# Instruction order and evacuation engines chosen per instruction, in a long-convolution and MLP kernel

## The chip, the cores and the metric

The kernel runs on one core of one Trainium2 chip. The metric is the device time of one launch in microseconds (us). A profile's span, from the first to the last instruction, is about 1.8 us shorter than the launch's time. All runs quoted here were in the fast state, and all gave the reference's result.

The names in the profiles: PE multiplies matrices, and PEld loads its weights; DVE, ACT and POOL work on vectors (ACT also computes the GELUs); SP issues most transfers, and SPq is its queue. SBUF is the core's working memory, and PSUM takes what PE writes. An evacuation is the copy of a result from PSUM to SBUF. A slab is 128 rows of the sequence. The granted clock is the share of its full speed that PE was allowed.

## The reference, cut to what matters

Sequence S = 2048, width D = 512, MLP width F = 1376, bf16.

```python
def A(q, k, v, shift_k, ssm_k, ssm_D):           # gated long convolution
    kv = shift_conv_4_taps(k, shift_k) * v
    y = irfft(rfft(pad(kv)) * rfft(pad(ssm_k)))[:S]
    return q * (y + kv * ssm_D)                  # y does not depend on q
def B(x): return gelu(layernorm(x) @ w1 + b1) @ w2 + b2

x = A_q
for layer in range(2):
    x = x + A(layernorm(x), k, v, ...)
    x = x + B(layernorm(x))
```

The convolution y is the same in both layers, so the kernel computes it once. Then come two layers of norms and MLP, all of them bound to PE.

## The kernel before

The program is recorded as a list of numbered operations. A list scheduler then fixes each engine's order (and the PSUM banks) before launch, from assumed durations. A last pass adds the semaphore waits. Operations carry tags: `ht` (transpose of the filter), `h1`, `h2` (the filter's transform, two stages), `fir*` (the four-tap convolution), `x1`, `x2` (transform of kv and the products of the spectra), `i1`, `i2` (inverse transform, two stages), `q`, `y`, `z` (norms and gate), `m1`, `m2` (MLP).

The scheduler's choice, cut:

```python
            o.ready = 0.0
    ...
            o.prio = o.base + o.extra + self.BIAS.get(o.tag, 0.0) + ...
    ...
            for e in free:                       # the five engines
                for o in ready[e]:
                    s = max(free[e], o.ready)    # and a free PSUM pair
                    k = (s + (self.SHY.get(o.tag, 300.0) if e == DVE and len(o.engs) > 1
                              and o.dur[DVE] > o.dur[ACT] else 0.0), -o.prio, o.i)
```

An evacuation of PSUM may run on ACT or on DVE (`BOTH`). The part that the argument turns on is the filter's spectrum, its copies and the products:

```python
    for k8 in range(16):                         # tag h2
        tl = stage2(R_G, range(8 * k8, 8 * k8 + 8), 128)      # 8 matmuls, 128 columns
        evac(BOTH, A(0, 128, R_H + 32 * k8, [4, 8], [512, 32], [1, 4]), ..., E1, tl)
    for d0, n in PARTS:                          # channels 0-63, then 64-127 of each block
        for g in range(2):
            for c in range(0, 128 * n, 2048):    # 16 copies of 256 KB, SBUF to SBUF
                src, dst = ...                   # partition halves swapped
                dma(dst, src, 1 << 18, reads=[src], rate=210.0)
    ...
            tt(h, x, h, ALU.mult, 30 + 1.09 * w) # a product: reads the spectrum and its copy
```

Each of the 16 h2 evacuations writes some columns of every channel, so each of the 16 copies reads what all 16 evacuations wrote.

## Time and profile before

| | us |
|---|---|
| time, median (lowest to highest, 3 runs; a fourth came with the result) | 247.12 (246.87 to 247.75) |
| span of the profiled run | 245.5 |
| first copy issued (end of h2) | 39.49 |
| second eight products start / end on DVE | 63.63 / 72.80 |
| inverse 2 starts on PE | 80.69 |
| first MLP matmul | 89.06 |
| last addition on DVE starts, lasts | 242.48, 0.69 |

The times from the first copy on are the joints of the chain: what lies between two of them can be compared from kernel to kernel even where the instructions are in another order. Two views that the prediction does not show follow. The first is DVE's order of time (start, duration, instructions, and in brackets the idle time before them with what ended it), at the second products:

```profile
63.63 9.17 DVE L513 TENSOR_TENSOR ar<-ar 128x2048 bf16<-128x2048 bf16 x8 [1.18 <-DMA ar<-ar]
```

DVE waits 1.18 us for a copy: up to there the copies, not DVE, set the pace. The second is PE's order of time where the convolution ends (L790 inverse 2, L884 the transposes of the first slab, L897 the MLP):

```profile
83.75 4.09 PE L790 MATMUL ps<-ar 128*128 128x256 bf16 x36
87.92 0.62 PE L884 MATMUL ps<-ar 128*128 128x128 bf16 x8
89.06 2.41 PE L897 MATMUL ps<-ar 128*128 128x128 bf16 x40 [0.52 <-DVE ar L519]
```

Here PE does two slabs' transposes in one piece after inverse 2, then waits 0.52 us for their evacuation on DVE.

### The profile page before, as it was taken

What the parts mean: (1) busy time and instruction counts of PE and PEld (TensorE: products, weight loads), DVE (VectorE), ACT (ScalarE), POOL (GpSimd) and SP (SyncE); (2) the same over time, 40 slices, a digit from 0 to 9 for tenths busy, and PEclk for the clock granted to TensorE, in tenths of its full rate; (3) what the DMA queues carried; (4) which work ended last, traced back from release to release, by engine and by line L of the source; (5) the groups of instructions that cost most, each with busy time, mean ns of one, the idle gap of its engine ahead of it and who ended that gap; (6) DMA issues with size and microseconds to landing.
All of it is one profiled execution on the core that took longest, in us unless ns stands there. A gap on an engine that the chain in (4) does not pass through costs nothing.

```text
span 245.5 us, 5643 instructions
## 1 busy us (share of the span) xinstructions
PE 228.3 (93%) x2382; PEld 154.6 (63%) x2399; DVE 175.1 (71%) x361; ACT 140.9 (57%) x222; POOL 34.1 (14%) x71
## 2 busy tenths in 40 slices
PE   7968789896799989999999999999999999999994
PEld 3857779785689878776586666744444444444443
DVE  0759999999898898889999967998687203002233
ACT  2297898999898997665455343633265130872000
POOL 2320002000003031232231111102121000000000
PEclk9999999999999999999999999999999999999999
DMA  6999923999996000420222023101520501101112
GB/s 240 372 408 406 406 47 82 215 212 212 346 396 198 0 3 0 45 43 3 46 43 43 3 41 67 24 1 21 101 53 0 109 19 43 45 0 43 43 45 85
DMA packets 25770, 27.68 MB, mean 113 GB/s; under 512 B 17585, under 2 KB 19984, under 8 KB 25616
## 3 DMA queue, kind: packets, MB, share of 16 engines
q1 hardware_dynamic: 25598, 27.21, 37.8%
q8 instruction: 19, 0.31, 0.5%
q10 hardware_dynamic: 146, 0.10, 0.2%
q14 instruction: 7, 0.06, 0.1%
HBM read 17.34 MB, written 2.10 MB: 79 GB/s over the span
## 4 chain that ended last, share of the span: by engine, by line
PE 64%; DVE 12%; SPq 8%; DMA 8%; issue 2%; ACT 2%; POOL 1%
PE ps L897 31%; PE ps L930 30%; SPq L502 8%; DVE ar L513 8%; DMA ar<-in_A_k_dram 5%; DMA ar<-ar 3%; DVE ar L519 2%; ACT ar L518 2%; PE ps L734 1%; PE ps L919 1%; POOL sm L830 1%; DVE sm L822 1%; PE ps L790 1%; DVE ar L672 1%; PE ps L623 0%
## 5 line engine op out<-in xcount | busy, mean ns | idle before, releaser
L902 ACT ACTIVATE ar<-ps,sm 128x256 bf16<-128x256 f32 (+5 forms) x143 | 67.1, 524 | 69.5 <-PE ps L930 55.1
L897 PE MATMUL ps<-ar 128*128 128x256 bf16 (+4 forms) x569 | 79.7, 297 | 0.7 <-DVE ar L519 0.5
L930 PE MATMUL ps<-ar 128*128 128x512 bf16 (+1 forms) x327 | 74.4, 379 | 0.7
L518 ACT ACTIVATE ar<-ps 128x1024 bf16<-128x1024 f32 (+1 forms) x76 | 71.4, 1038 | 6.4 <-PE ps L610 2.9
L897 PEld LDWEIGHTS ps<-ar 128*128 128x128 bf16 (+1 forms) x572 | 53.2, 100 | 26.9 <-DVE ar L519 0.7
L513 DVE TENSOR_TENSOR ar<-ar 128x512 bf16<-128x512 bf16 (+2 forms) x104 | 61.9, 642 | 3.3 <-DMA ar<-in_A_k_dram 1.8
L930 PEld LDWEIGHTS ps<-ar 128*128 128x128 bf16 (+1 forms) x341 | 33.2, 98 | 37.5
L934 DVE TENSOR_TENSOR ar<-ar,ps 128x512 bf16<-128x512 bf16 x31 | 20.6, 681 | 44.8 <-PE ps L930 44.8
L822 DVE BATCH_NORM_STATS2 sm<-ar 128x6 f32<-128x512 bf16 (+1 forms) x68 | 41.8, 647 | 0.0
L837 DVE TENSOR_SCALAR ar<-ar,sm 128x512 bf16<-128x512 bf16 x64 | 23.5, 403 | 8.6 <-POOL sm L830 8.6
L830 POOL TENSOR_TENSOR sm<-sm 128x2 f32<-128x2 f32 (+2 forms) x26 | 20.2, 778 | 2.2
L610 PE MATMUL ps<-ar 128*64 128x128 bf16 x512 | 17.7, 221 | 2.7 <-ACT ar L518 1.9
L519 DVE CAST ar<-ps 128x1024 bf16<-128x1024 f32 (+1 forms) x16 | 17.9, 1149 | 3.1 <-PE ps L610 1.6
L828 POOL TENSOR_SCALAR sm<-sm 128x2 f32<-128x2 f32 (+2 forms) x26 | 5.7, 218 | 92.2 <-DVE sm L824 92.0
L734 PE MATMUL ps<-ar 128*128 128x128 bf16 x256 | 15.3, 220 | 3.0 <-DVE ar L513 1.6
L610 PEld LDWEIGHTS ps<-ar 128*64 128x64 bf16 x512 | 14.8, 110 | 5.1 <-ACT ar L518 3.0
L734 PEld LDWEIGHTS ps<-ar 128*128 128x128 bf16 x256 | 14.6, 114 | 3.6 <-DVE ar L513 1.7
L519 DVE COPY ar<-ps 128x2048 bf16<-128x2048 bf16 (+1 forms) x8 | 7.1, 917 | 6.8 <-PE ps L593 6.8
L710 PE MATMUL ps<-ar 128*128 128x64 bf16 x256 | 9.4, 193 | 1.9 <-ACT ar L518 1.1
L824 DVE BATCH_NORM_AGGREGATE sm<-sm 128x2 f32<-128x6 f32 (+1 forms) x64 | 10.3, 173 | 0.2
L710 PEld LDWEIGHTS ps<-ar 128*128 128x128 bf16 x256 | 8.1, 98 | 3.1 <-ACT ar L518 2.2
L623 PE MATMUL ps<-ar 128*128 128x128 bf16 x128 | 8.4, 220 | 1.5 <-ACT ar L518 1.0
(30 smaller groups left out, 77.5 us busy)
## 6 DMA issues: line engine op xcount, KB each, us to landing
ar<-tab_s SPq DMA_DIRECT2D x8, 512.0 KB, 16.1
ar<-ar SPq DMA_DIRECT2D x16, 256.0 KB, 6.5
ar<-in_A_ssm_k_dram SPq DMA_DIRECT2D x4, 512.0 KB, 5.4
ar<-in_A_k_dram SPq DMA_DIRECT2D x4, 512.0 KB, 10.1
ar<-in_A_v_dram SPq DMA_DIRECT2D x4, 512.0 KB, 13.6
ar<-in_A_q_dram SPq DMA_DIRECT2D x4, 512.0 KB, 9.0
out_dram<-ar SPq DMA_DIRECT2D x7, 256.0 KB, 2.0
ar<-in_B_w_dram SPq DMA_DIRECT2D x1, 1376.0 KB, 12.5
```

The costliest lines, as they stand in the source:

```text
L513: return P.op(eng, lambda e: e.tensor_tensor(o, a, b, op), dur, reads=[a, b] + list(more), writes=[o])
L518: return e.activation(dst, src(), AF.Copy)
L519: return e.tensor_copy(dst, src())
L610: r = e.matmul(Q(tl, 64 * ri, 64, i * 128, [1, 128]), w, m, start=True, stop=True)
L734: r = e.matmul(Q(tl, 0, 128, i * 128, [1, 128]), w, m, start=q == 0, stop=q == 1)
L822: P.op(DVE, lambda e, sj=sj, x=x: e.bn_stats(sj, x), 40.0 + 1.1 * w, reads=[x], writes=[sj], gate=gate)
L830: P.op(POOL, lambda e: e.tensor_tensor(r, v, hf, ALU.pow), 430.0 + 150.0 * n, reads=[v, hf], writes=[r])
L837: P.op(DVE, lambda e: e.tensor_scalar(o, x, m, r, ALU.subtract, ALU.mult), 335.0, reads=[x, m, r], writes=[o])
L897: r = e.matmul(Q(tl, 0, rows, 0, [1, w]), a, m, start=dk == 0, stop=dk == 3)
L902: P.op(ACT, lambda e, dst=dst, tl=tl, rows=rows, bias=bias, w=w: e.activation(dst, Q(tl, 0, rows, 0, [1, w]), AF.Gelu_apprx_tanh, bias=bia ...
L930: r = e.matmul(Q(tl, 0, 128, 0, [1, 512]), ins[fc][0], ins[fc][1], start=fc == 0, stop=fc == 10)
L934: P.op(DVE, lambda e, x=x, tl=tl: e.tensor_tensor(x, x, Q(tl, 0, 128, 0, [1, 512]), ALU.add), 640.0, reads=[x], writes=[x], tile=tl)
```

## The change

The intent is a shorter schedule from the same operations: a search gave single operations a correction of priority of their own (`PB`, 944 of them), a reluctance to go to DVE (`PS`, 12), an earliest start (`HOLD`, 316) or the engine (`ENG`, 62). The scheduler's assumed DMA latency also changes. The core of the diff; the tables run to over a thousand numbers and are cut:

```diff
-    BIAS = {'fir0': 47900, 'fir1': -42700, ...}
-    SHY = {'fir0': 1000, 'fir1': 150, 'h1': 950, ...}
+    BIAS = {'': 534647, 'fir0': -142308, 'fir1': 3955434, ...}
+    SHY = {'fir0': 0, 'fir1': 7, 'h1': 0, ...}
+    PB = {0: -999765647, 1: -1000017924, ...}       # by operation number
+    PS = {59: 197, 69: 25, 77: 1264, ...}
+    HOLD = {7: 6449, 9: 11403, ...}
+    ENG = {37: ('vector',), 43: ('vector',), 49: ('scalar',), ...}
-            o.ready = 0.0
+            o.ready = self.HOLD.get(o.i, 0.0)
+            o.allow = self.ENG.get(o.i, o.engs)
-            o.prio = o.base + o.extra + self.BIAS.get(o.tag, 0.0) + (...)
+            o.prio = o.base + o.extra + self.BIAS.get(o.tag, 0.0) + self.PB.get(o.i, 0.0) + (...)
-                    k = (s + (self.SHY.get(o.tag, 300.0) if e == DVE and ... > o.dur[ACT] else 0.0), -o.prio, o.i)
+                    k = (s + (self.PS.get(o.i, self.SHY.get(o.tag, 300.0)) if e == DVE and ... > o.dur.get(ACT, 1e9) else 0.0), -o.prio, o.i)
-                o.end = dma_free + 1900.0
+                o.end = dma_free + 2300.0
(and o.engs becomes o.allow where the ready lists are filled and emptied)
```

## The prediction

> **What bounds the kernel now.** I read the table of stretches first, because the page's shares average over stages with different limits: the convolution (to about 89 us) and the two MLP layers after it.
>
> ```profile
> span 245.5 us, 5643 instructions
> PE 228.3 (93%) x2382; PEld 154.6 (63%) x2399; DVE 175.1 (71%) x361; ACT 140.9 (57%) x222; POOL 34.1 (14%) x71
> ```
>
> ```profile
> core 0: us, PE busy (x) PEld busy (x) DVE busy (x) ACT busy (x) POOL busy (x), PEclk, DMA share, GB/s
> 0.00:17.40 17.40, 13.89 (x232) 10.53 (x232) 7.17 (x6) 8.10 (x10) 5.86 (x15) 1.00 0.88 336
> 17.40:39.50 22.10, 19.04 (x352) 17.09 (x352) 22.06 (x20) 18.83 (x19) 1.30 (x2) 1.00 0.70 258
> 39.50:63.60 24.10, 19.57 (x519) 16.91 (x517) 22.80 (x20) 22.57 (x24) 0.52 (x1) 1.00 0.97 207
> ...
> 97.00:130.00 33.00, 32.79 (x237) 23.52 (x240) 30.93 (x90) 17.72 (x41) 9.56 (x20) 1.00 0.21 33
> 130.00:170.00 40.00, 39.79 (x248) 24.64 (x251) 35.95 (x100) 19.30 (x44) 6.73 (x12) 1.00 0.14 27
> 170.00:210.00 40.00, 39.84 (x184) 18.26 (x185) 19.15 (x49) 13.87 (x22) 3.72 (x6) 1.00 0.24 54
> 210.00:242.50 32.50, 32.22 (x157) 15.72 (x159) 6.22 (x11) 10.29 (x16) 0.00 (x0) 1.00 0.12 42
> ```
>
> From 97 us on PE is busy 32.79 + 39.79 + 39.84 + 32.22 = 144.64 of 145.5 us: no order of the same matmuls can win more than 0.9 us there. Before 89 us no engine is full throughout, but DVE (22.06 of 22.10) and then ACT are full in turn. What ties them together is in the chain of waits:
>
> ```profile
> 5.78 11.63 DMA ar<-in_A_k_dram
> ...
> 34.59 1.08 PE ps L623 x16
> ...
> 35.69 3.78 ACT ar L518 x4
> ...
> 39.49 0.55 SPq L502
> ...
> 55.92 7.69 DMA ar<-ar
> ...
> 63.63 9.17 DVE ar L513 x8
> ```
>
> The reader should see five links. The k load sets the start of the FIR work on DVE at 17.44. The last evacuation of the filter's spectrum (tag h2) ends on ACT at 39.47. Only then can SP issue the 16 copies of the spectrum, for each of them reads what all 16 evacuations wrote. From 39.49 to the release of DVE at 63.63 it is 24.14 us of issuing and flight. Then come the second eight products on DVE, to 72.8, the inverse transforms on PE, and at 89.06 the first MLP matmul:
>
> ```profile
> 77.98 2.87 PE ps L734 x48
> 80.85 1.32 PE ps L790 x12
> ...
> 89.06 2.41 PE ps L897 x40
> ```
>
> After that the chain is PE to the end, 153.4 us. So the time is (end of h2) + 24.1 + 9.2 + (inverse, norm of the first slab: 89.06 - 72.80 = 16.3) + 153.4 + (last addition and store: about 3).
>
> How much air lies before the end of h2 is shown by ACT's order of time:
>
> ```profile
> 10.59 1.26 ACT L540 ACTIVATE ar<-ar 128x512 bf16<-128x512 bf16 x2 [7.53 <-DMA ar<-in_A_shift_k_dram]
> 11.76 6.49 ACT L518 ACTIVATE ar<-ps 128x1024 bf16<-128x1024 f32 x7
> 18.56 4.62 ACT L518 ACTIVATE ar<-ps 128x2048 bf16<-128x2048 bf16 x4 [0.32 <-PE ps L653]
> 24.85 3.77 ACT L518 ACTIVATE ar<-ps 128x1024 bf16<-128x1024 f32 x4 [1.67 <-PE ps L610]
> 29.34 3.77 ACT L518 ACTIVATE ar<-ps 128x1024 bf16<-128x1024 f32 x4 [0.71 <-PE ps L623]
> 33.43 6.03 ACT L518 ACTIVATE ar<-ps 128x1024 bf16<-128x1024 f32 x6 [0.32 <-PE ps L623]
> ```
>
> ACT waits 0.32 + 1.67 + 0.71 + 0.32 = 3.0 us between 10.59 and 39.46; its work there is 25.9 us. DVE in its own order of time waits 6.64 us at the start and 0.17 + 0.73 + 0.92 + 1.81 = 3.6 us more before 17.44.
>
> **What the Trainium skill says.** "Perfetto Trace Analysis", section Optimization Strategy: where the most contended engine changes over time, look for the gaps within each regime and for what ends them, and interleave regimes. The trace agrees that there are regimes (table above). The same page, What "DMA-bound" means: an issuing sequencer that is solid with DMA slices is bound by making descriptors, not by moving data. Here SP issues the 16 copies in 17.66 us, back to back, about 1.1 us each, so this part does not shrink with another order. "VectorE: DVE Perf Modes", The perf-mode tier table: a copy with a PSUM operand is at most 2x for bf16 and, by the section on why PSUM drops a tier, 1x for fp32. The trace agrees: on DVE 2048 bf16 take 1218 ns and 1024 fp32 take 1215 ns. ACT has no such gain: 1877 ns for 2048 bf16 against 0.94 us per 1024 fp32 in a row (3.77 / 4). So a 2048 bf16 evacuation is dear on ACT and a 1024 fp32 one is slightly cheaper there.
>
> **The change, part by part.** No operation is added, removed or resized; the tables only change the priorities, earliest starts and permitted engines of the list scheduler that fixes each engine's order before launch. Its own earliest-start numbers cost nothing on the chip: what runs is the order and the waits. I compared the two built programs' orders. PE has the same 2401 matmuls in another order (84 runs of equal ones become 124). DVE goes from 363 instructions to 362, ACT from 226 to 227. SP issues all loads in the same order; only the last stores differ.
>
> 1. *Until the end of h2.* Four of the 16 h1 evacuations go to DVE instead of two, and they stand ahead of the FIR, where DVE waited 3.6 us; one 2048 bf16 FIR transpose evacuation moves from DVE to ACT; h2 goes from 6 on DVE and 10 on ACT to 5 and 11. ACT's work ahead of its last h2 evacuation: 25.9 - 2 x 0.943 + (4.62 - 3 x 0.943 = 1.79) + 0.943 = 26.7 us. It still begins with the copy that waits for the shift load (10.59). PE's order now spreads the h1 groups around the FIR matmuls (three after the first transposes, three after the first FIR group), which answers the 1.67 us wait. One wait stays: eight ACT items stand ahead of the transpose evacuation, done at 10.59 + 1.26 + 6 x 0.943 = 17.5, but the transposes start with the k load at 17.46 and end at 18.5, so 1.0 us. End of h2: 10.59 + 26.7 + 1.0 = 38.3 at the best. DVE has two instructions fewer between 17.44 and its last h2 evacuation (39.17 - 2 x 1.13 = 36.9), so ACT comes last. **-1.2 us.**
> 2. *Copies and products.* 24.1 + 9.2 unchanged. DVE reaches the second products 2.3 us earlier, the data only 1.2: its wait there (1.18 before) grows to about 2.3. **0**, and half of what DVE saved is lost here.
> 3. *Inverse 1.* Eight groups of the second part can start only after the last product. Before: 72.80 to 80.85, 8.05 us; 48 matmuls take 2.87, so 8 x 0.957 = 7.65 without waits. DVE takes three of these evacuations (before two), placed straight after the products. **-0.4.**
> 4. *Inverse 2 to the first MLP matmul.* Before, PE ends inverse 2 at 87.84 and starts the MLP at 89.06. After, one slab's transposes lie inside inverse 2, and the two z evacuations move from DVE to ACT. On DVE, 12 us of work lie between the products and that slab's norm. With the products ending at 71.6 and a wait for the fourth group of part 2 (about 1.6 us), it is done at about 85.3, when PE is about to finish inverse 2 (71.6 + 7.65 + 7.15 = 86.4). First MLP matmul about 86.6 to 86.8. **-0.9.**
> 5. *The MLP.* The same matmuls, no air: at most -0.9. Against it: ACT now does four evacuations beside 22 GELUs of the first two slabs, about 1.7 + 22 x 0.27 = 7.6 of 8.4 us, where PE before waited for nothing; and m1 and m2 alternate more finely, each with a wait. **+0.5.**
> 6. *The end.* The last PE group is a 256-wide half (11 matmuls, addition of 0.42 us, 64 KB) instead of a 512-wide group (0.69 us, 128 KB). **-0.3.**
>
> Sum: -1.2 - 0.4 - 0.9 + 0.5 - 0.3 = -2.3 us: 247.1 - 2.3 = 244.8.
>
> **Rivals.** (a) *More comes through.* If ACT lost its 1.0 us wait too, h2 would end at 37.3 and all later stages keep it; with the 0.9 us of the MLP and no +0.5 the sum is -4.7, or 242.4. For it: DVE would be ready at 36.9. Against: the k load stands where it stood, and PE gets a PSUM pair for the second FIR group only when DVE has done five FIR operations and an evacuation (about 24.4). (b) *Gain eaten by new waits.* The order was fixed from assumed durations; an engine works in order, so one mistaken duration blocks what stands behind. Candidates: the inverse evacuations that DVE takes ahead of the statistics (the products end early, but the group isn't ready), additions of m2 standing ahead of norms, and PE's finer alternation. PE would show gaps between 87 and 130 us. 0.5 to 1 us each, so 245.5 to 247. (c) *Contention.* The copies start 1.2 us earlier but after all loads have landed, and every stretch has a granted clock of 1.00; I expect no change of it.
>
> **Range and chances.** 243.2 to 246.5. 2% is 4.9 us; that asks for the whole of (a) and a bit more, and since neither the copies, the products nor the MLP can shrink, I give it 0.06. Slower by 2% would need 7 us of new waits after a search that kept the total work: 0.02.
>
> **What would show it.** Step 1: the end of the last h2 evacuation (SP's first copy) at 38.3 instead of 39.5. Step 2: DVE's wait for the copies about 2 us, the distance of 24.1 unchanged. Steps 3 and 4: the first MLP matmul at 86 to 87. Step 5: from there 153 to 154 us to the last matmul. Step 6: a last addition of 0.42 us. I am wrong if the copies start at 39.5 or before 37.5, if the 24.1 changes, or if PE shows more than 1 us of gaps after its first MLP matmul.

## The result, and the profile after

| | median us (lowest to highest, runs) | ratio to before, 95% |
|---|---|---|
| before | 247.13 (246.87 to 247.75, 4) | |
| after | 245.55 (245.24 to 246.23, 4) | 0.9936 (0.9908 to 0.9964) |
| after, measured again | 245.34 (244.36 to 246.88, 6) | 0.9912 (0.9879 to 0.9946) |

A ratio is the mean time of one kernel's fast runs over that of the other's of the same rounds, so it is not quite the ratio of the medians. The change wins 0.6 to 0.9%, 1.6 to 2.2 us, well inside the 2% that counts as the same.

The page of the kernel after, its span, busy times and the granted clock by slices of a fortieth of the span:

```profile
span 243.5 us, 5664 instructions
...
PE 230.0 (94%) x2399; PEld 156.4 (64%) x2399; DVE 178.8 (73%) x360; ACT 142.8 (59%) x223; POOL 33.2 (14%) x71
...
PEclk9999999999799999999999999999999999999999
```

One slice, from 61 to 67 us, has a lower clock: PE's order of time below has 48 matmuls in 4.50 us there, which in the chain of before took 2.87. PE's busy time is 1.7 us longer than before on the same matmuls, but that need not all come from this dip: the trace of before lacks 17 matmul records, and a kernel below without a dip (convolution old, rest new) has 229.9 us. The stretches of the kernel after, cut at its own joints (columns: length, then busy time and count of PE, PEld, DVE, ACT, POOL, then clock, DMA share, GB/s):

```profile
core 0: us, PE busy (x) PEld busy (x) DVE busy (x) ACT busy (x) POOL busy (x), PEclk, DMA share, GB/s
0.00:38.30 38.30, 32.66 (x584) 27.93 (x584) 29.88 (x26) 27.55 (x28) 6.22 (x17) 1.00 0.81 301
38.30:62.90 24.60, 20.00 (x516) 17.48 (x514) 22.36 (x21) 22.63 (x24) 0.00 (x0) 0.97 0.97 207
62.90:87.40 24.50, 23.96 (x363) 22.36 (x361) 22.35 (x42) 22.67 (x26) 5.22 (x12) 0.96 0.56 208
87.40:240.90 153.50, 153.42 (x946) 88.62 (x943) 103.83 (x273) 69.94 (x146) 21.71 (x42) 1.00 0.17 36
```

The stretches were 39.5, 24.1, 25.4 and 153.4 us before. So the first wins 1.2 us, the second loses 0.4, the third wins 0.9, and the MLP is as long as it was, with PE full in it.

The chain of waits of the kernel after, at the same links:

```profile
24.39 13.88 ACT ar L658 x14
38.28 0.55 SPq L642
...
54.05 7.06 DMA ar<-ar
61.24 4.50 PE ps L874 x48
...
239.66 1.22 PE ps L1059 x11
240.90 0.42 DVE ar L1063
```

The way to the first copy now ends in 14 ACT evacuations back to back, where before it ran along DVE from 17.44 to 34.54 and only then over PE to four ACT evacuations. After the copies the chain runs over the slow 48 matmuls and not over the second products, but only just: PE was done with the first part of inverse 1 at 72.07, and the second products ended at 72.04. The last link is the 0.42 us addition. ACT's order of time ahead of the copies:

```profile
13.59 3.94 ACT L658 ACTIVATE ar<-ps 128x1024 bf16<-128x1024 f32 x4
18.75 19.50 ACT L658 ACTIVATE ar<-ps 128x2048 bf16<-128x2048 bf16 x19 [1.22 <-PE ps L793]
```

One wait of 1.22 us, for the first FIR transposes, is left of the four that summed to 3.0 us. From 18.75 to 38.25 ACT works without a gap. DVE's order of time, at the two groups of eight products:

```profile
52.01 9.17 DVE L653 TENSOR_TENSOR ar<-ar 128x2048 bf16<-128x2048 bf16 x8 [0.46 <-DMA ar<-ar]
62.86 9.18 DVE L653 TENSOR_TENSOR ar<-ar 128x2048 bf16<-128x2048 bf16 x8 [1.68 <-DMA ar<-ar]
```

DVE is early for both groups and waits 0.46 + 1.68 = 2.14 us for copies, against 1.18 before. PE's order of time from the inverse transform to the MLP (L874 inverse 1, L930 inverse 2, L1024 a slab's transposes, L1037 the MLP):

```profile
61.24 4.50 PE L874 MATMUL ps<-ar 128*128 128x128 bf16 x48 [1.60 <-DVE ar L653]
...
79.33 6.76 PE L930 MATMUL ps<-ar 128*128 128x256 bf16 x60
86.08 0.40 PE L1024 MATMUL ps<-ar 128*128 128x128 bf16 x4
86.31 0.60 PE L930 MATMUL ps<-ar 128*128 128x256 bf16 x4
87.14 0.40 PE L1024 MATMUL ps<-ar 128*128 128x128 bf16 x4 [0.23 <-DVE ar L977]
87.37 1.95 PE L1037 MATMUL ps<-ar 128*128 128x128 bf16 x32
```

The first slab's transposes do stand inside inverse 2, only four matmuls before its end. The second slab's come after it, 0.23 us late, and the MLP follows without the 0.52 us wait.

The budget, from the joints: end of h2 39.49 to 38.28, -1.21. Copies, 24.14 to 24.58, +0.44. Products, 9.17 and 9.18, 0. End of products to inverse 2, 7.89 to 7.29, -0.60. Inverse 2 to the MLP, 8.37 to 8.04, -0.33. MLP to the last addition, 153.42 to 153.53, +0.11. From there to the end of the span, 3.0 to 2.6, -0.4. The sum is -2.0, as the spans say (245.5 to 243.5).

### The profile page after: what moved, and what is told of

Read it like the earlier page. It is cut to its first block, busy times and chain, and to the rows that moved or that the text cites. A ratio compares the mean times of both kernels' runs of the same rounds, so it can differ in the third digit from the quotient of the medians.

```text
span 243.5 us, 5664 instructions
## 1 busy us (share of the span) xinstructions
PE 230.0 (94%) x2399; PEld 156.4 (64%) x2399; DVE 178.8 (73%) x360; ACT 142.8 (59%) x223; POOL 33.2 (14%) x71
## 2 busy tenths in 40 slices
DMA packets 25770, 27.68 MB, mean 114 GB/s; under 512 B 17585, under 2 KB 19984, under 8 KB 25616
## 4 chain that ended last, share of the span: by engine, by line
PE 69%; SPq 8%; DMA 8%; ACT 7%; DVE 5%; issue 1%; POOL 0%; DVEq 0%
PE ps L1037 30%; PE ps L1070 29%; SPq L642 8%; ACT ar L658 7%; PE ps L874 6%; DMA ar<-in_A_k_dram 5%; DMA ar<-ar 3%; DVE sm L962 2%; DVE ar L653 1%; PE ps L1059 1%; PE ps L805 1%; DVE ar L659 1%; PE ps L930 1%; PE ps L750 1%; DVE sm L964 0%
## 5 line engine op out<-in xcount | busy, mean ns | idle before, releaser
L1042 ACT ACTIVATE ar<-ps,sm 128x256 bf16<-128x256 f32 (+3 forms) x143 | 68.8, 522 | 67.5 <-PE ps L1037 40.1
L1037 PE MATMUL ps<-ar 128*128 128x256 bf16 (+4 forms) x572 | 82.4, 297 | 0.0
L1070 PE MATMUL ps<-ar 128*128 128x512 bf16 (+1 forms) x341 | 79.6, 379 | 0.0
L658 ACT ACTIVATE ar<-ps 128x1024 bf16<-128x1024 f32 (+3 forms) x77 | 71.9, 1032 | 5.3 <-PE ps L874 2.1
L1037 PEld LDWEIGHTS ps<-ar 128*128 128x128 bf16 (+1 forms) x572 | 53.3, 100 | 28.4 <-ACT ar L658 0.3
L653 DVE TENSOR_TENSOR ar<-ar 128x512 bf16<-128x512 bf16 (+2 forms) x104 | 63.4, 644 | 3.0 <-DMA ar<-ar 2.1
L962 DVE BATCH_NORM_STATS2 sm<-ar 128x6 f32<-128x512 bf16 (+1 forms) x68 | 43.0, 651 | 0.4
L659 DVE CAST ar<-ps 128x1024 bf16<-128x1024 f32 (+1 forms) x18 | 20.8, 1190 | 2.2 <-PE ps L874 1.1
L874 PE MATMUL ps<-ar 128*128 128x128 bf16 x256 | 16.7, 231 | 1.9 <-DVE ar L653 1.6
L874 PEld LDWEIGHTS ps<-ar 128*128 128x128 bf16 x256 | 16.1, 118 | 2.3 <-DVE ar L653 1.7
L659 DVE COPY ar<-ps 128x2048 bf16<-128x2048 bf16 (+1 forms) x5 | 5.2, 1063 | 7.3 <-PE ps L733 7.3
L850 PEld LDWEIGHTS ps<-ar 128*128 128x128 bf16 x256 | 8.2, 98 | 3.2 <-ACT ar L658 2.9
L763 PE MATMUL ps<-ar 128*128 128x128 bf16 x128 | 8.0, 220 | 0.8 <-ACT ar L658 0.8
```

The source lines that it names most:

```text
L653: return P.op(eng, lambda e: e.tensor_tensor(o, a, b, op), dur, reads=[a, b] + list(more), writes=[o])
L658: return e.activation(dst, src(), AF.Copy)
L659: return e.tensor_copy(dst, src())
L874: r = e.matmul(Q(tl, 0, 128, i * 128, [1, 128]), w, m, start=q == 0, stop=q == 1)
L962: P.op(DVE, lambda e, sj=sj, x=x: e.bn_stats(sj, x), 40.0 + 1.1 * w, reads=[x], writes=[sj], gate=gate)
L1037: r = e.matmul(Q(tl, 0, rows, 0, [1, w]), a, m, start=dk == 0, stop=dk == 3)
```

## The experiments

The tool of most experiments is a replay. The kernel before got two tables, each engine's list of operation numbers and each tile's PSUM banks, and its scheduler was made to take the next of the list instead of choosing:

```diff
+    ORDER = {'tensor': [33, 36, 39, ...], 'scalar': [...], ...}
+    BASE = {33: [0], 36: [2], ...}
-                for o in ready[e]:
-                    if o.eng is not None or any(g.eng is None for g in o.gate):
+                nx = len(self.order[e])
+                if nx >= len(self.ORDER[e]): continue
+                for o in [ops[self.ORDER[e][nx]]]:
+                    if o.npred or any(g.eng is None for g in o.gate):
-            for b in range(0, 8, pool.nb):
+            for b in self.BASE.get(i, range(0, 8, pool.nb)):
```

With one kernel's lists the replay is that kernel again, instruction by instruction (only the order within some lists of waits differs). With edited lists one part of the change can be had alone. The joints of all profiled runs:

| kernel | first copy | 2nd products | from copy | products end | first MLP matmul | span |
|---|---|---|---|---|---|---|
| before | 39.49 | 63.63 | 24.14 | 72.80 | 89.06 | 245.5 |
| before, replayed | 39.49 | 63.81 | 24.32 | 72.99 | 89.24 | 245.6 |
| after | 38.28 | 62.86 | 24.58 | 72.04 | 87.37 | 243.5 |
| after, again | 38.24 | 62.54 | 24.30 | 71.71 | 87.04 | 243.1 |
| after, replayed | 38.06 | 62.52 | 24.46 | 71.69 | 87.03 | 243.1 |
| convolution new, rest old | 38.05 | 62.48 | 24.43 | 71.66 | 87.92 | 244.3 |
| convolution old, rest new | 39.49 | 64.09 | 24.60 | 73.26 | 88.71 | 244.8 |
| engines new, order old | 40.60 | 65.05 | 24.45 | 74.22 | 90.5 | 247.2 |
| filler | 37.86 | 61.91 | 24.05 | 71.09 | 86.42 | 242.5 |
| 8 copies | 38.08 | 61.74 | 23.66 | 71.69 | 87.56 | 243.6 |
| old, halves | 35.08 | no wait | | 71.71 | 87.96 | 244.3 |
| new, halves | 39.21 | no wait | | 74.34 | 90.08 | 246.1 |
| new, halves, reordered | 36.35 | no wait | | 70.59 | 86.31 | 242.4 |
| new, halves, earlier still | 35.46 | no wait | | 70.78 | 87.64 | 243.5 |

The theory was the prediction's: the gain comes from three separate places (the end of h2, the passage from the products to the MLP, the last group), it adds up, and the copies pass the first on unchanged. The rivals were that one place carries it all, that the dip in the clock eats part of it, and that order and engine choice could be had apart.

### Half the change each way

The change to the convolution alone (everything up to the products), with the rest of the old order; and the reverse. Lists were exchanged place by place, and the PSUM pairs of x2, i1 and i2 were left to the scheduler.

```diff
 # convolution new, rest old: PE's list (the other engines' likewise)
-33,36,39,42,45,48,50,52,54,56,58,60,62,64,66,128,68,70,130,132,...   then the old rest
+33,36,39,42,48,50,52,45,70,56,54,62,74,64,76,128,66,78,72,132,...   then the old rest
 # convolution old, rest new: the first line, then the new rest
```

> The engines' orders are fixed by hand: everything up to the second transform of the products (loads, h1, h2, FIR, x1, x2) in the new order and on the new engines, everything after it (both inverse transforms and the MLP) in the old. Theory 1, the gain is made in three places: the end of h2 comes 1.2 us earlier, but about 0.45 us of it is lost again between the copies' start and the second products, so this kernel keeps 0.8 of the 1.6 us: 246.3 us, last h2 evacuation at 38.3, products' end at 72.0, first MLP matmul at 88.3. Theory 2, all of the gain is made ahead of the copies and the rest is neutral: 245.5 us. Theory 3, the gain lies in the transition and the end alone: 247.1 us.

> The reverse: up to the second transform of the products in the old order, the rest in the new. Theory 1: no gain at the end of h2 (39.5), but the inverse transforms, the transition to the MLP (0.7 us) and the shorter last group and store (0.4 us) remain: 246.0 to 246.3 us, first MLP matmul about 88.3. Theory 2: 247.1 us. Theory 3: 245.5 us.

Measured: convolution new 246.12 (245.07 to 247.5, 14 runs), 0.9939 (0.9917 to 0.9961). Rest new 246.48 (245.84 to 247.7, 13 runs), 0.9942 (0.9922 to 0.9963). The kernel before, in the same rounds: 247.58. The lines of SP's own queue show what the first hybrid took over, first of the convolution new, then of the convolution old (start, duration of all issues):

```profile
38.05 17.47 SPq L507 DMA_DIRECT2D ar<-ar  x16
```

```profile
39.49 17.70 SPq L507 DMA_DIRECT2D ar<-ar  x16
```

The first copy moves with the convolution's half alone. From the end of the products to the MLP it is 16.26 us with the old rest, exactly as before, and 15.45 with the new rest. By their spans the halves are worth 1.2 and 0.7 us, together 1.9 of the 2.0 to 2.4 us of the whole in its three traces. So each half wins without the other, and in the traces they add up. The timed runs say this less sharply: by the ratios the halves win 1.5 and 1.4 us, together 1.2%, and the whole 0.64, 0.88 and 0.95%; the intervals just allow that to be equal.

### The same program again

No edit to the kernel after in the first of these; the replays of both kernels, with their own lists, are the other two.

> The changed kernel itself once more. Its instruction-by-instruction replay gave 0.9905 at a clock of 1.00, its own first four runs 0.9936, all at a mean clock of 0.993. If the difference is of the chip or the session, this run and the replay agree, 0.990 to 0.992. If the lower clock comes again and costs time, 0.9936 and a clock of 0.993 in the same stretch.

> A control: the kernel before, replayed from fixed lists. Ratio 1.000. A second trace of it: first copy at 39.5, and the distance from there to the second products, 24.14 in the first trace and 24.0 to 24.6 in all others, shows how far this stretch varies by itself.

> A control: the changed kernel's own engines, order and PSUM banks, replayed from fixed lists instead of found by the list scheduler. The built programs are the same instruction by instruction, waits included. It should give the changed kernel's time, 245.5 us (ratio 0.9936), and narrow its interval, which rests on four runs so far. If the two halves of the change were additive (0.9939 and 0.9942, each against the kernel before), it would be 0.988, 244.2 us; if the lower clock that the changed kernel shows in one stretch costs time, or the copies land later there than in the hybrids, it stays at 0.9936.

Measured: after again 245.34, as in the table above; before replayed 247.4 (246.84 to 248.08, 20 runs), 0.9984 (0.9972 to 0.9996); after replayed 244.98 (244.52 to 245.76, 6 runs), 0.9905 (0.9881 to 0.9929). The replay is a fair tool, to about 0.2%. The clock tells something as well. PE's order of time, replay of the kernel after, whose profiled run had a clock of 1.000:

```profile
61.35 2.87 PE L739 MATMUL ps<-ar 128*128 128x128 bf16 x48 [1.71 <-DVE ar L518]
```

These are the 48 matmuls that took 4.50 us in the first trace of the kernel after. The repeat of the kernel after had the dip too (clock 0.993, 4.31 us), yet the repeat and the replay have the same span, 243.1, and the same first MLP matmul, 87.04 and 87.03. In both, PE goes on with the second part of inverse 1 when the second products end: the lost time was lost ahead of that wait. The dip is not the new order's either, for the replay of the kernel before had it in the same slice (span 245.6, against 245.5 at 1.000).

Over all timed runs it looks less clean. In 94 runs of the kernel before, 40 had a mean clock below 0.998; on the three chips that ran them their mean span was 0.4 us longer, the same, and 0.2 us longer than that of the others. Of the program after, the replay's two such runs were 0.2 us shorter than its other four, and the repeat's four were 1.3 us longer than its other two. It looks clean in three of the four kernels below that leave DVE no wait for copies. "Old, halves": two runs at 0.993 took 247.0 us, the eight at 1.000 took 245.9 to 246.2. "New, halves": 247.7 to 248.3 at 0.993, 248.7 to 249.1 at 0.985 and 0.986, 250.1 to 250.4 at 0.979 and below. "Earlier still": 246.8 and 246.9 at 0.993, 245.2 to 245.3 at 1.000. There a lower clock goes with 0.9 to 1.7 us more a step. In the fourth, "reordered", the one run at 0.993 is no longer than the others. And steps of about 1 us come without it too: the six runs of the filler below, all at 1.000, are four at 244.3 to 244.7 and two at 245.4 and 245.5. Runs other than the profiled one have no trace, so it is unknown where in them the clock fell. All four runs of the first measurement had a clock of 0.992 or 0.993; whether some of its 245.55 comes from that stays open.

### Filling PE's wait before inverse 1

To see whether PE's idle time ahead of the dip matters, 24 matmuls of zeros were put in front of inverse 1's first group, into the tile that the group then overwrites.

```diff
+            if d8 == 6:                          # first group in PE's order
+                for i in range(24):              # one operation
+                    e.matmul(Q(tl, 0, 128, 0, [1, 128]), zeros, zeros, start=True, stop=True)
```

> The changed kernel with 24 matmuls of zeros put on PE where it waits 1.6 us for the first products, into the PSUM pair of the group that follows. Question: does the drop of the granted clock between 62 and 68 us (48 inverse matmuls take 4.50 us instead of 2.87) come from that wait, and does it cost time? If it comes from the wait, the clock is 1.00 throughout and the 48 take 2.9 us. Theory A: the drop is off the path, as PE still ends these groups when the second products end (72.07 against 71.95): 245.5 us, at most 0.2 less. Theory B: it costs its 1.6 us, or a good part: 244.0 to 244.7 us.

Measured: 244.57 (244.28 to 245.47, 6 runs), 0.9893 (0.9868 to 0.9917); clock 1.000 in all six runs, span 242.5. The profiled run is 0.6 us ahead of the replay that ran on the same chip. The table shows where: its first copy is 0.20 earlier and its copies 0.41 shorter, and neither waits for the filler. Six runs without a dip against two dips in six of the replay do not show that the filler prevents it, and the ratios of filler and replay overlap. No effect of it is shown.

### The new engines in the old order

The evacuations of the convolution on the engines of the new kernel, PE's order as before, PSUM pairs left to the scheduler.

```diff
 PE: 33,36,39,42,45,48,50,...                     as before
-ACT: 9,10,49,51,53,57,61,63,65,129,67,69,71,73,75,77,79,81,83,87,...
+ACT: 9,10,49,53,55,59,61,129,67,69,71,73,75,77,79,143,81,85,87,89,...
-DVE: 37,40,43,46,55,59,156,157,172,...
+DVE: 37,40,43,46,51,57,63,65,156,157,172,...
```

> The kernel before in its own PE order; only the engine choice up to the end of h2 is the new one (four h1 evacuations on DVE ahead of the FIR instead of two, one FIR transpose evacuation on ACT, h2 5 and 11). Theory 'order and engines together': ACT has the 26.7 us of work of the new kernel but keeps about 3 us of waits for PE, so the last h2 evacuation ends at 39.5 to 40.3, no earlier than before: 247.0 to 248.0 us. Rival 'the engine choice alone does it': 38.0 to 38.5 and 246.1 us.

Measured: 248.48 (247.93 to 249.61, 14 runs), 1.0026 (1.001 to 1.0042), slower than before. The first copy is issued at 40.60, 1.1 us later than before and later than any theory expected. ACT's order of time says why:

```profile
11.48 4.64 ACT L523 ACTIVATE ar<-ps 128x1024 bf16<-128x1024 f32 x5
18.66 4.62 ACT L523 ACTIVATE ar<-ps 128x2048 bf16<-128x2048 bf16 x4 [2.54 <-PE ps L658]
24.95 15.62 ACT L523 ACTIVATE ar<-ps 128x1024 bf16<-128x1024 f32 x16 [1.66 <-PE ps L615]
```

With more of h1 on DVE, ACT is done with its share by 16.1 and waits 2.54 us for the FIR transposes, then 1.66 us for h1 groups that PE has put behind the FIR matmuls. Taking work off ACT became waiting. In the kernel after ACT waits 1.22 us in the first place and not at all in the second, where PE runs three h1 groups after the first transposes and three after the first FIR group. So the engines alone don't give the h2 gain. Whether the new order alone would, with the old engines, was not run; that it takes both is the likely reading.

### Copies of double size

The prediction had said that making descriptors on SP bounds the copies. Half as many copies of double size halve the number of issues.

```diff
-            for c in range(0, 128 * n, 2048):
+            for c in range(0, 128 * n, 4096):    # rows of 4096 elements, 8 copies
-                dma(dst, src, 1 << 18, ...)
+                dma(dst, src, 1 << 19, ...)
```

> The changed kernel with the 4 MB of spectrum copied in 8 transfers of 512 KB instead of 16 of 256 KB. My prediction said that SP's descriptor making bounds the copies (17.7 us for 16 issues, about 1.1 us each). If the number of issues binds, the distance from the first copy to the second products falls from 24.6 to about 15 us, DVE's 1.7 us wait vanishes and the time falls to 244. Rival: the 16 DMA engines bind (their busy share in this stretch is 0.92 to 0.97), SP is only held back by full queues: the distance stays at 24 to 25 us, each issue takes about twice as long, and the time stays within 0.5 us of 245.5.

Measured: 245.27 (243.88 to 245.8, 6 runs), 0.9895 (0.9863 to 0.9927), the same as the replay's 0.9905. Its six runs spread widely, though: two, at 243.88 and 243.99, are the shortest of the whole study, and the profiled one, at 245.45, is of the slower four. SP's own queue, with 8 copies and then with 16 (the kernel after):

```profile
38.08 15.09 SPq L507 DMA_DIRECT2D ar<-ar  x8
```

```profile
38.28 17.85 SPq L642 DMA_DIRECT2D ar<-ar  x16
```

An issue went from 1.1 to 1.9 us. Were SP's work on an issue the bound, 8 issues would have taken about 8.9 us. A cost per packet would have shown too: the rows are half as many and twice as long, and the page counts 640 packets fewer (25130 against 25770). A cost on SP by the byte is not excluded by this run. The way from the first copy to the second products shrank by 0.4 to 0.9 us only (23.66 against 24.05 to 24.60), and nothing of that reached the end, since DVE then waited for ACT (0.65, 0.22 and 0.39 us). The table of stretches of the kernel after has a DMA share of 0.97 there. So with the DMA engines near full, it is most likely the transfers that bind, and SP looks solid because it is held up behind them. What limits the transfers was not tested: in the kernel before, the DMA engines moved 207 GB/s in the stretch of the copies, at a share of 0.97, and 336 GB/s ahead of 17.4 us, at 0.88. Each copy runs between 64 of the 128 partitions; a copy over all of them was not tried. PE also had two gaps of 1.71 and 1.56 us there which the profile puts down to nothing; they stay unexplained.

### Copies that need not wait for all of h2

If the end of h2 and the copies are what sets the pace, the dependence is the lever. Here h2 is cut by channels: eight groups give channels 0 to 63 of each block, eight give the rest, and the first eight copies read only what the first eight evacuations wrote. PE does 256 matmuls of 64 columns instead of 128 of 128.

```diff
-    for k8 in range(16):
-        tl = stage2(R_G, range(8 * k8, 8 * k8 + 8), 128)
-        evac(BOTH, A(0, 128, R_H + 32 * k8, [4, 8], [512, 32], [1, 4]), ...)
+    for d0, n in PARTS:
+        for k16 in range(8):                     # 16 matmuls of 64 columns each
+            evac(BOTH, A(0, 128, R_H + 128 * d0 + 64 * k16, [4, 16], [512, 16], [1, 4]), ...)
```

> The same halves of h2 in the kernel before. Theory 1: here DVE waited only 1.18 us for copies, because it had 2.3 us more to do; so it can win only about 1.1 us, 246.0 us, and the distance between the two orders grows from 1.6 to over 2 us. Rival: the copies are off the path here: 247.1 us.

> The changed kernel's order, but the h2 matmuls are done in two halves of 64 columns instead of 16 groups over all 128, so that the first eight copies of the spectrum need only the first eight evacuations. Same evacuations, same copies. If the copies are what holds the second products (Theory 1, half of what DVE saved is lost in waiting for them): SP issues its first copy at about 34.5 instead of 38.3, DVE's waits of 0.46 and 1.68 us for copies vanish, products end at 69.9 instead of 72.0, and the time falls by 1.3 to 2 us to 243.5 to 244.2. Rival: the inverse transform is paced by ACT's evacuations and PE anyway, the products' end doesn't carry through: 245.2 to 245.5 us.

Measured: with the old order 246.13 (245.87 to 247.04, 10 runs), 0.9937 (0.9913 to 0.996). With the new order 248.73 (247.7 to 250.37, 22 runs), 1.0045 (1.0025 to 1.0065). DVE's order of time, halves in the old order:

```profile
53.46 18.25 DVE L518 TENSOR_TENSOR ar<-ar 128x2048 bf16<-128x2048 bf16 x16
```

All 16 products run in one piece: the 1.2 us of waiting for copies are gone, and the span is 1.2 us shorter. So the copies are on the path of the kernel before, by as much as DVE waits for them. The new order failed for a reason of its own. PE's order of time:

```profile
30.35 0.64 PE L645 MATMUL ps<-ar 128*128 128x64 bf16 x16 [1.83 <-DMA ar<-tab_s]
...
33.16 4.99 PE L645 MATMUL ps<-ar 128*128 128x64 bf16 x112 [2.17 <-DMA ar<-tab_s]
```

The first half of h2 now needs all of the transform's table early, and the new order of groups (80, 84, 82, 90, 94, ...) asked for two of its blocks before they had landed. Right after the second wait PE's clock fell too, to 0.50 from 34 to 37 us, in the midst of these matmuls. The new order was tuned to the arrival of its data, and here a change of the work made it stale; the old order took the same change without harm.

The groups were then put in the order in which the table lands, with groups of the second half in between. Which evacuations go to DVE was chosen anew, five as before.

```diff
 # h2 groups in PE's order (80-94 first half, 96-110 second half)
-80,84,82,90,94,86,92,96,98,88,100,102,106,104,108,110
+80,82,84,86,88,96,90,98,100,92,102,94,104,106,108,110
 # and, in "earlier still", with the PSUM pairs chosen anew:
+80,82,84,86,88,90,96,92,98,94,100,...
```

> h2 in halves again in the new order, now asking for the blocks of the large table in the order in which they land; the first trial asked for blocks 5 and 7 early, and PE waited 4.0 us for them. Theory 1 (copies on the path): first copy issued at about 35.3, no wait of DVE for copies, products end at about 70.0, first MLP matmul 85.4 to 86.0; 243.5 to 244.2 us. Rival: ACT's evacuations pace the inverse transforms, so the earlier products' end is lost: 245.2 to 245.5.

> h2 in halves with the first half's groups placed as soon as the table's blocks land, and PSUM pairs chosen anew, since in the last trial PE waited 1.0 us for ACT ahead of the first half's last group. First copy at 34.9 instead of 36.35, last h2 evacuation at 38.2 instead of 39.06, products' end 69.8 instead of 70.5; 243.7 us, ratio 0.985. Rival: with no wait for copies left, DVE's own work and ACT's evacuations set the pace, and it stays at 0.987.

Measured: reordered 244.34 (244.22 to 244.39, 4 runs), 0.9874 (0.985 to 0.9899); earlier still 245.24 (245.15 to 246.93, 6 runs), 0.9921 (0.9891 to 0.995). DVE's order of time, halves reordered:

```profile
52.33 18.26 DVE L518 TENSOR_TENSOR ar<-ar 128x2048 bf16<-128x2048 bf16 x16
```

No wait for copies is left in it, where the replay that ran on the same chip had 0.80 + 1.23 = 2.03 us. The products end 1.1 us earlier (70.59 against 71.69). The other 0.9 us went to work ahead of the products, which DVE reaches at 52.33, against 51.32 in the replay: PE waited 0.99 us for an ACT evacuation before the first half's last group, and DVE 0.47 + 0.25 us for h2 and FIR groups. Then 0.4 us more is lost up to the MLP (15.72 us from the products' end, against 15.34), where PE of the replay waits 0.38 us for the second products, this kernel's PE does not wait, so its own work sets the pace. Its runs do not overlap with the replay's on the same chip (244.22 to 244.39 against 244.52 to 245.76), though the two intervals do. By median and ratio it is the fastest kernel of the study, 1.3% ahead of before; with four runs against steps of about 1 us its lead over the replay is not certain.

With the copies earlier still (35.46) the products ended no earlier (70.78): DVE reached them at 52.53 and did not wait for a copy. The newly chosen PSUM pairs also cost a wait at the start of the MLP, in PE's order of time:

```profile
87.41 0.40 PE L898 MATMUL ps<-ar 128*128 128x128 bf16 x4 [1.35 <-DVE ar L524]
```

## Why the prediction was right, point by point

The time, 245.55, lies in the range and 0.75 above the number; the two later measurements lie nearer to it (-2.2 and -2.3 us by their ratios, against the predicted -2.3). The terms of the sum are not all as right as the sum, and that their misses partly cancel is luck. Two of the prediction's own signs of being wrong came up in the first trace: the 24.1 changed, to 24.58, and the first MLP matmul came at 87.37, outside 86 to 87. One reading was loose: between 39.5 and 63.6 us it is not ACT that is full after DVE; DVE is busy 22.80 us there and ACT 22.57.

1. **End of h2: -1.2 predicted, -1.21 measured** (38.3 against 38.28). The working held, also in its rest: the wait for the FIR transposes was put at 1.0 and was 1.22. Rival (a), in which this wait goes too, did not come true.
2. **Copies and products: 0 predicted, +0.44 measured** in that trace. DVE's wait of about 2.3 us before the second products came out at 1.68 there, and 0.46 before the first, together 2.14. The distance of the copies is not a constant: over the nine traces in which 16 copies were released all at once it lay between 24.05 and 24.60, and before, replayed, had 24.32. So the change did not lengthen the copies by a mechanism that could be shown; the kernel before was read on the short side of a scatter. The reason given for the fixed length, descriptor making on SP, does not hold: with half the issues and half the rows the way stayed nearly as long, so the transfers are most likely the limit.
3. **Inverse 1: -0.4 predicted, -0.6 measured.** The 7.65 us "without waits" was too long: 0.957 us per group came from a piece of 48 matmuls with the end of its last one in it. In the replay the 128 matmuls of the eight groups take 7.15 us from their start to that of what follows.
4. **Inverse 2 to the MLP: -0.9 predicted, -0.33 measured.** This is the term that was sized worst. The step took the moved transposes as free. They still cost PE its time, 0.23 us, inside inverse 2; and the second slab's stand after it and wait 0.23 us for the norm on DVE. What was saved is the wait for the evacuation and the shorter piece of transposes.
5. **The MLP: +0.5 predicted, +0.1 measured.** The feared waits on ACT did not come. PE is busy 153.42 of 153.50 us in that stretch, and the only wait of size is the 0.23 us just before it. Terms 4 and 5 were off by about the same, in opposite directions.
6. **The end: -0.3 predicted, -0.4 measured,** with the addition of 0.42 us.

Rival (b), new waits that eat the gain, was not seen in the kernel after, but it was seen at once where an order was used for work it was not made for (engines new in the old order, halves in the new order). Of rival (c) the prediction said that the clock would not change. It did, in the trace of the kernel after. In the traces of that kernel it cost next to nothing, since it fell ahead of a wait for the products; what it costs in runs without a trace, and why it comes in some runs of either kernel, stays open.

## What to carry to other kernels

Judge a new order by the link that ends last at each joint, not by busy shares: by the page the change made DVE busy for 3.7 us more, and the kernel was faster, above all because the last evacuation ahead of the copies came 1.2 us earlier. An evacuation moved to another engine pays only if PE's order keeps both engines fed: here the same move cost 1.1 us at the first copy with the old order and came with a gain of 1.2 us in the new. Where many transfers wait for the last of many writers, cut the work so that the first transfers need only the first writers: in the old order that won 1.5 us, against 1.6 to 2.4 us of the whole search. An order that was tuned to the arrival of its data may then have to be fitted again, as the new one had to be.

## What the Trainium skill lacked or had wrong

- "TensorE: Matmul & The Clock Gate", Back-to-back issue gap, says that a sustained stream takes about 131 ns per matmul at 512 columns and 81 ns at 128, and that the isolated formula (216 and 56 ns) is off. The runs show the opposite. In PE's order of time of the kernel after, 47 matmuls of 512 columns take 10.16 us from the first to the start of what follows, 216 ns each; in the replay, 128 of 128 columns take 7.15 us, 56 ns each.

```profile
229.34 10.33 PE L1070 MATMUL ps<-ar 128*128 128x512 bf16 x47
239.50 1.37 PE L1059 MATMUL ps<-ar 128*128 128x256 bf16 x11
```

- "Perfetto Trace Analysis", What "DMA-bound" means, reads a solid issuing queue as the making of descriptors. Here SP was solid for 17.7 us with 16 issues and 15.1 us with 8 of double size, with the DMA engines' share at 0.97, so it was more likely held up by the transfers. The page names both limits but does not say how to tell which one binds where the queue and the engines both look full; halving the number of issues is a test.
